# Seven half-size products in place of eight in the last six feed-forward blocks, and a ring of four batches for their input

## The chip, the core and the metric

The kernel runs on one core of a Trainium2 chip. The metric is the device time of one execution in microseconds (us), the median of several runs; the profiled span is about 1.8 us shorter than the time of the same run. A ratio is the mean time of one kernel's runs over the mean of the other's runs of the same rounds, so it isn't quite the ratio of the medians quoted.

PE is TensorE, DVE is VectorE, ACT is ScalarE, POOL is GpSimd and SP is SyncE. SBUF and PSUM are the two on-chip memories; here a PSUM bank holds one result of 128 x 512 fp32. In a line of a profile, `o<-ps_f` means that o is written from ps_f, `L714` is the line of kernel.py, and `[2.70 <-PE ...]` is the idle time before the instruction and what ended it.

## The reference

```python
# attention: batch 8, heads 8, sequence 576, head size 64
scores = scale * np.matmul(q, k.transpose(0, 1, 3, 2))
mask_local = (rel >= 0) & (rel < 32)                        # heads 0 to 3
mask_strided = (rel >= 0) & (pos[None, :] % 32 == pos[:, None] % 32)   # heads 4 to 7
... # softmax over the keys, then
x = np.matmul(attn, v) # as 4608 tokens x 512
# feed-forward: 4608 tokens, model size 512, inner size 2048
h = x @ w_in
r = np.maximum(h, 0.0)
g = s * (r * r) + b
out = g @ w_out           # fp32
```

## The kernel before

The tokens are worked in nine blocks (numbered 0 to 8) of 512. A planner emits the instructions of all engines in one order, and each engine keeps to it: in the traces below a TensorE or VectorE instruction that waits holds up all behind it (5.24 us in one case). The scores and sums of attention are used as filler between feed-forward matmuls. The second product of a block is 64 matmuls of 512 columns. Each 16 of them fill one PSUM bank, VectorE evicts it into one of three output buffers, and SyncE stores that buffer:

```python
op = ctx.enter_context(tc.tile_pool(name="op", bufs=3))      # output buffers, 2 KB a partition each
xT = [const.tile([128, NTOK], FP16, name=f"xT{i}") for i in range(4)]
...
def ff2(T, ts, ft, group, part=0, parts=1):
    ...
        nc.tensor.matmul(
            out=gts[id_], lhsT=gts[T][:, ft, ts * 128:(ts + 1) * 128],
            rhs=w_out_sb[:, ft, cols], start=(ft == 0), stop=(ft == NFT - 1))
    ...
        def ev(eng):
            o = op.tile([128, DM], FP32, tag="o", name="o")
            nc.vector.scalar_tensor_tensor(
                out=o[:, 0:n], in0=gts[id_], scalar=s_sb[:, 0:1], in1=bcs[:, cols],
                op0=ALU.mult, op1=ALU.add)
            r0 = T * PS + ts * 128
            nc.sync.dma_start(out=out[r0:r0 + 128, cols], in_=o[:, 0:n])
```

Attention of a head pair needs q and k transposed, which in the later batches SyncE does by DMA in the same queue as the stores.

The softmax here doesn't subtract the row's maximum and nothing guards it: scores larger than these inputs give would overflow.

## Time and profile before

| | before |
|---|---|
| median of the first 3 runs (a fourth came with the result) | 318.59 us (317.58 to 319.23) |
| profiled span | 315.9 us |
| TensorE busy | 310.1 us, 98% |
| VectorE busy | 194.5 us, 62% |
| granted TensorE clock | 1.00 in every stretch |

A busy share of 98% says that TensorE is nearly always occupied, so the first question for a change is what it does to TensorE's stream of matmuls, and the second is whether any other engine can make TensorE stop. The lines of the page are shown and read in the prediction.

### The profile page before, as it was taken

The page shows a single profiled execution, that of the slowest core. Times are in us where ns is not written, and L with a number is a line of the kernel's source. Part 1 is how long each engine was busy: PE and PEld are TensorE (multiplying, and loading weights), DVE is VectorE, ACT ScalarE, POOL GpSimd, SP SyncE. Part 2 cuts the span into 40 slices and gives each one's busy share as a digit, 9 for nine tenths or more (in the row PEclk, how much of TensorE's full clock was granted, in tenths as well). Part 3 has the DMA queues.
Part 4 walks back from the last instruction along what each step waited for, and adds up shares of the span by engine and source line. Part 5 has one row for each costly group of instructions (what it writes and reads, how often), then busy time and mean ns, then how long its engine had stood idle before and what let it go on. Part 6 is the DMA issues. An engine that isn't in the chain of part 4 may idle for free.

```text
span 315.9 us, 6151 instructions
## 1 busy us (share of the span) xinstructions
PE 310.1 (98%) x2268; PEld 175.2 (55%) x2268; DVE 194.5 (62%) x543; ACT 160.8 (51%) x304; POOL 97.1 (31%) x140
## 2 busy tenths in 40 slices
PE   8999999999999999999999999999999999999995
PEld 3775655666556566556555655565544454544444
DVE  5576868798967797658566877595732254333212
ACT  1776944788838688547037815661531164333100
POOL 8562569902960292059201870000000000000000
PEclk9999999999999999999999999999999999999999
DMA  8999999994999699679997999923050100100021
GB/s 128 206 212 204 212 170 152 233 139 97 78 156 170 84 139 141 129 141 135 159 187 145 122 164 147 165 89 106 19 91 33 66 35 0 66 36 33 33 100 70
DMA packets 99385, 37.83 MB, mean 120 GB/s; under 512 B 82394, under 2 KB 93274, under 8 KB 99354
## 3 DMA queue, kind: packets, MB, share of 16 engines
q0 software_dynamic: 57200, 18.08, 57.8%
q1 hardware_dynamic: 42154, 19.35, 31.5%
q8 instruction: 18, 0.29, 0.4%
q14 instruction: 13, 0.11, 0.1%
HBM read 36.84 MB, written 10.62 MB: 150 GB/s over the span
## 4 chain that ended last, share of the span: by engine, by line
PE 89%; DMA 8%; POOL 1%; issue 0%; SPq 0%; DVE 0%; POOLq 0%
PE ps_f L703 39%; PE ps_f L663 37%; PE ps_s L505 5%; DMA kl<-in_k_dram 4%; PE ps_a L557 4%; DMA w_out_sb<-in_v_dram 2%; DMA ql<-in_q_dram 2%; PE ps_t L387 1%; PE ps_a L726 1%; PE ps_t L605 1%; POOL v_loc L293 1%; PE ps_f L557 0%; SPq L797 0%; POOL ql L251 0%; PE ps_f L387 0%
## 5 line engine op out<-in xcount | busy, mean ns | idle before, releaser
L663 PE MATMUL ps_f<-xT,w_in_sb 128*128 128x512 f16 x568 | 145.7, 379 | 0.0
L703 PE MATMUL ps_f<-w_out_sb,gT 128*128 128x512 f16 (+1 forms) x592 | 144.8, 373 | 0.0
L681 ACT ACTIVATE u<-ps_f 128x512 f16<-128x512 f32 x140 | 82.8, 597 | 98.3 <-PE ps_f L663 85.0
L687 DVE TENSOR_TENSOR gT<-u 128x512 f16<-128x512 f16 x144 | 59.5, 417 | 46.9 <-ACT u L681 46.0
L663 PEld LDWEIGHTS <-w_in_sb 128*128 128x128 f16 x576 | 61.2, 114 | 44.6 <-issue 0.2
L703 PEld LDWEIGHTS <-gT 128*128 128x128 f16 x592 | 55.6, 98 | 52.5 <-DVE gT L687 0.6
L519 ACT ACTIVATE pt<-ps_s 128x384 f16<-128x384 f32 (+2 forms) x92 | 42.0, 490 | 8.1 <-PE ps_s L505 7.3
L714 DVE SCALAR_TENSOR_TENSOR o<-ps_f,s_sb,bcs 128x512 f32<-128x512 f32 (+1 forms) x37 | 27.0, 730 | 25.1 <-PE ps_f L703 24.5
L557 PEld LDWEIGHTS <-pt 72*72 72x72 f16 (+1 forms) x448 | 31.8, 119 | 15.9
L583 DVE TENSOR_TENSOR x_nat<-ps_a,rec 72x256 f16<-72x256 f32 (+1 forms) x76 | 35.0, 460 | 1.3
L572 DVE RECIPROCAL rec<-ps_a 72x4 f32<-72x4 f32 (+1 forms) x76 | 13.8, 181 | 24.3 <-PE ps_a L557 24.1
L271 POOL DMA_DIRECT2D v_loc<-in_v_dram x28 | 20.6, 742 | 3.7 <-DVE qD_loc L293 2.3
L758 POOL COPY gate<-kT 1x1 f16<-1x1 f16 x6 | 1.4, 230 | 47.6 <-DMA kT<-ks 47.6
L527 DVE TENSOR_TENSOR pt<-pt,mask_str 72x432 f16<-72x432 f16 (+1 forms) x42 | 14.6, 356 | 1.8 <-ACT pt L519 1.3
L527 DVE TENSOR_TENSOR pt<-pt,mask_loc 128x384 f16<-128x384 f16 x42 | 14.0, 352 | 2.4 <-ACT pt L519 2.0
L557 PE MATMUL ps_a<-v_str,pt 72*72 72x65 f16 x204 | 15.3, 197 | 0.0
L276 POOL DMA_DIRECT2D v_str<-in_v_dram x16 | 13.0, 816 | 5.6 <-DVE rec L572 2.7
L557 PE MATMUL ps_a<-v_loc,pt 128*96 128x65 f16 x150 | 12.0, 206 | 0.0
L248 POOL DMA_DIRECT2D kl<-in_k_dram x16 | 11.7, 745 | 0.0
L913 PE MATMUL ps_f<-ones 128*128 128x512 f16 (+2 forms) x30 | 9.3, 444 | 1.4 <-DVE ones L226 1.1
L505 PE MATMUL ps_s<-qD_loc,kT_loc 128*128 128x192 f16 x68 | 10.4, 246 | 0.0
L293 ACT COPY xT<-ps_t 128x576 f16<-128x576 f16 x7 | 4.5, 638 | 10.9 <-PE ps_t L605 10.9
(111 smaller groups left out, 242.5 us busy)
## 6 DMA issues: line engine op xcount, KB each, us to landing
out_dram<-o SPq DMA_DIRECT2D x35, 256.0 KB, 4.2
w_out_sb<-in_moe_w_out_dram POOLq DMA_DIRECT2D x4, 512.0 KB, 10.8
v_loc<-in_v_dram POOLq DMA_DIRECT2D x28, 72.0 KB, 7.9
ql<-in_q_dram POOLq DMA_DIRECT2D x6, 288.0 KB, 6.9
qs<-in_q_dram POOLq DMA_DIRECT2D x6, 288.0 KB, 5.1
ks<-in_k_dram POOLq DMA_DIRECT2D x6, 288.0 KB, 6.9
kl<-in_k_dram POOLq DMA_DIRECT2D x4, 288.0 KB, 8.8
kl<-in_k_dram POOLq DMA_DIRECT2D x16, 72.0 KB, 4.0
```

What stands on the lines that cost most here:

```text
L271: nc.gpsimd.dma_start(out=vl[LPAD:128, h, :, 0:D], in_=v_band(b, h))
L505: nc.tensor.matmul(out=st["s", g][0:nk, c:c + 2 * nq], lhsT=(st["k"][:, i * nq:i * nq + nk] if loc else st["k"][:, i, 0:SQ]), rhs=st["q"][ ...
L519: nc.scalar.activation(out=pt[0:nk, 0:2 * n].rearrange("k t c -> k (t c)"), in_=st["s", g][0:nk, 0:2 * n * nq], func=AF.Exp, scale=scale)
L527: nc.vector.tensor_tensor(out=pt[0:nk, 0:2 * n], in0=pt[0:nk, 0:2 * n], in1=mask, op=ALU.mult)
L557: nc.tensor.matmul(out=st["a"][0:nq, j % per, :], lhsT=st["pt", g][0:nk, i, :], rhs=vt[0:nk, 2 * mm + e, j, :])
L572: nc.vector.reciprocal(out=st["rec", e, j][0:nq, 0:per], in_=st["pa", e, j][0:nq, 0:per, D:D + 1])
L583: nc.vector.tensor_tensor(out=st["x"][:, j0:j0 + per, 64 * e:64 * e + 64], in0=st["pa", e, j][0:nq, 0:per, 0:D], in1=st["rec", e, j][0:nq, ...
L663: nc.tensor.matmul(out=gts["h", T, ft], lhsT=w_in_sb[min(ft // 4, 2)][:, ct].rearrange("p (c x l) -> p c l x", x=128, l=4)[:, max(ft // 4 ...
L681: nc.scalar.activation(out=gts["u", T, ft], in_=gts["h", T, ft], func=AF.Relu)
L687: nc.vector.tensor_tensor(out=gts[T][:, ft, :], in0=u, in1=u, op=ALU.mult)
L703: nc.tensor.matmul(out=gts[id_], lhsT=gts[T][:, ft, ts * 128:(ts + 1) * 128], rhs=w_out_sb[:, ft, cols], start=(ft == 0), stop=(ft == NFT ...
L714: nc.vector.scalar_tensor_tensor(out=o[:, 0:n], in0=gts[id_], scalar=s_sb[:, 0:1], in1=bcs[:, cols], op0=ALU.mult, op1=ALU.add)
```

## The change

Strassen's scheme writes a 2 x 2 block product with seven half-size products of sums in place of eight. For each of the last six blocks (3 to 8), the 64 matmuls of 512 columns become 7 x 16 of 256 columns. VectorE pays for it: sums of the activations g (in place, in fp16), four mixings of the weights once, and intermediate values (Va, Ua, Ub, Vb) that are copied out of PSUM between products. To make room in SBUF, the transposed x is kept for four batches in a ring and not for all eight, and some input buffers are shared.

```diff
+    sp = ctx.enter_context(tc.tile_pool(name="sp", bufs=1))
+    cp = ctx.enter_context(tc.tile_pool(name="cp", bufs=1))
+    w_mix = {i: const.tile([128, NFT // 2, DM // 2], FP16, name=f"w_mix{i}") for i in (2, 3, 4)}
-    xT = [const.tile([128, NTOK], FP16, name=f"xT{i}") for i in range(4)]
+    NX = 4
+    xT = [const.tile([128, NX * S], FP16, name=f"xT{i}") for i in range(4)]
...
-                                  bufs=7 if loc else 6, name="pt")
+                                  bufs=6, name="pt")
...
+    SEVEN = 3
+    def sums_post(T):
...
+            plan.post([("S", T, 1, h), ("P1", T)], ns,
+                      make((0, 0), (1, 0), (0, 0), ALU.subtract), [("S", T, 2, h)])
...
+        jobs = ((3, wr[1], wr[0]), (1, wr[0], wl[0]), (2, wr[1], w_mix[1]), (4, wl[1], w_mix[2]))
+        before = [("F2", SEVEN - 1)]
...
+        def store(i, k, of, plus, ts=slice(0, 2)):
+            def g(eng):
+                o = op.tile([128, 2, 256], FP32, tag="o", name="o")
+                nc.vector.scalar_tensor_tensor(
+                    out=o[:, ts], in0=gts[of, T][:, ts], scalar=s_sb[:, 0:1],
+                    in1=plus()[:, ts], op0=ALU.mult, op1=ALU.add)
+                r0 = T * PS + 256 * i
+                nc.sync.dma_start(...)
...
+        seq = [
+            ("P1", X, ..., [([d("P1"), ("bcs",)], EV, ev("Va", "X", lambda: b1), [d("Va")])]),
+            ("P5", W, ..., mix(1), sn(1), wait(1), []),
+            ("P2", X, ..., [d("Va")], [([d("P2")], EV, store(0, 0, "X", lambda: b1), [X])]),
+            ("P6", Y, ..., ev("Ua", ...), add_db -> Ub),
+            ("P7", Z, ..., ev("Vb", ...), store(1, 1, "W", val("Vb"))),
+            ("P4", Z, ..., [d("Vb")] + wait(4), store(1, 0, "Z", val("Ua"))),
+            ("P3", W, ..., [d("C22")], store(0, 1, "W", val("Ub"))),
+        ]
+        if not late:
+            seq = [seq[i] for i in (0, 2, 3, 4, 1, 5, 6)]
```

P1 to P7 are the seven products; C11, C22, C21 and C12 are the four quarters of a block's output, stored in that order. P2 accumulates into the bank that P1 filled, so it can't start before Va has been copied out of it.

## The prediction

> **What bounds the kernel now.** I read the page from the top: busy time of each engine, then the chain that ended last.
>
> ```profile
> PE 310.1 (98%) x2268; PEld 175.2 (55%) x2268; DVE 194.5 (62%) x543; ACT 160.8 (51%) x304; POOL 97.1 (31%) x140
> ...
> PE 89%; DMA 8%; POOL 1%; issue 0%; SPq 0%; DVE 0%; POOLq 0%
> PE ps_f L703 39%; PE ps_f L663 37%; PE ps_s L505 5%; DMA kl<-in_k_dram 4%; PE ps_a L557 4%; DMA w_out_sb<-in_v_dram 2%; DMA ql<-in_q_dram 2%; PE ps_t L387 1%; PE ps_a L726 1%; PE ps_t L605 1%; POOL v_loc L293 1%; PE ps_f L557 0%; SPq L797 0
> ```
>
> 89% of the chain is TensorE; the two feed-forward products are 76% of it, and VectorE has none. A busy PE need not stream, so I looked at the groups of the two products and at the last microseconds in the timeline.
>
> ```profile
> L663 PE MATMUL ps_f<-xT,w_in_sb 128*128 128x512 f16 x568 | 145.7, 379 | 0.0
> ...
> L703 PE MATMUL ps_f<-w_out_sb,gT 128*128 128x512 f16 (+1 forms) x592 | 144.8, 373 | 0.0
> ```
>
> ```profile
> 302.13 0.75 DVE L714 SCALAR_TENSOR_TENSOR o<-ps_f,s_sb,bcs 128x512 f32<-128x512 f32 x1 [2.70 <-PE ps_f L703]
> 305.58 0.75 DVE L714 SCALAR_TENSOR_TENSOR o<-ps_f,s_sb,bcs 128x512 f32<-128x512 f32 x1 [2.70 <-PE ps_f L703]
> 309.04 0.75 DVE L714 SCALAR_TENSOR_TENSOR o<-ps_f,s_sb,bcs 128x512 f32<-128x512 f32 x1 [2.70 <-PE ps_f L703]
> 310.79 0.48 DVE L714 SCALAR_TENSOR_TENSOR o<-ps_f,s_sb,bcs 128x256 f32<-128x256 f32 x1 [1.00 <-PE ps_f L703]
> 312.53 0.48 DVE L714 SCALAR_TENSOR_TENSOR o<-ps_f,s_sb,bcs 128x256 f32<-128x256 f32 x1 [1.26 <-PE ps_f L703]
> ```
>
> The idle column is 0.0: neither product waits. Evictions 3.46 us apart close 16 matmuls of 512 columns each: 216 ns a matmul. The last two are 1.74 us apart and close 16 of 256 columns: 109 ns each, although every one has a new stationary operand. So half-size products cost half. The PE order is therefore a clock: counting matmuls at 216, 109 and the shorter attention sizes gives when each step would run if nothing waited.
>
> Then VectorE by stretch, to see what room it has.
>
> ```profile
> 60.00:80.00 20.00, 20.00 (x181) 12.52 (x180) 17.81 (x49) 16.92 (x34) 6.31 (x10) 1.00 0.97 129
> 120.00:140.00 20.00, 20.00 (x147) 11.21 (x145) 13.61 (x42) 12.18 (x22) 3.25 (x8) 1.00 0.96 130
> 260.00:280.00 20.00, 20.00 (x95) 9.88 (x93) 7.37 (x16) 7.76 (x13) 0.00 (x0) 1.00 0.07 26
> ```
>
> The third figure after the length and the PE is DVE: up to 89% (17.81 of 20) without a PE gap, 68% in the middle, 37% late. The change adds where there is little room (120 to 200 us) as well as where there is much.
>
> Last, the attention cycle, which has one PSUM bank:
>
> ```profile
> 187.11 0.17 DVE L572 RECIPROCAL rec<-ps_a 72x4 f32<-72x4 f32 x1
> 187.32 0.42 DVE L583 TENSOR_TENSOR x_nat<-ps_a,rec 72x256 f16<-72x256 f32 x1
> ```
>
> Attention output takes PE 0.30 us, then 0.17 and 0.42 on DVE with small gaps, before the bank is free: about 1.0 us a group when nothing fills it. Today feed-forward matmuls fill it.
>
> **What the Trainium skill says.** "TensorE: Matmul & The Clock Gate", Back-to-back issue gap: columns/2.4 + 2.5 ns, so 216 at 512 and 109 at 256; the trace agrees exactly. Same page, Part 3, The mechanism: matmuls are strictly in order, so one that waits for a bank holds all behind it; the before trace has no such wait to show it. "VectorE: DVE Perf Modes", The perf-mode tier table: a 16-bit tensor_tensor from SBUF runs two elements a cycle, fp32 or PSUM one. The trace agrees: squares of 512 take 417 ns and masks of 384 take 352, a slope of 0.51 to 0.56 ns an element; the 512-column eviction takes 744.
>
> **The change, part by part.**
>
> PE: six blocks lose 64 x 216 = 13.82 us and get 7 x 16 x 109 = 12.21: 1.62 a block, 9.7 in all. One block's first product straddles the ring of four batches and becomes 128 halves: +0.1. Gain 9.6 us.
>
> DVE: a sum of 1024 fp16 elements is 0.71 us (417 + 512 x 0.56); the trace's adjacent instructions overlap by some 0.07, so it occupies 0.64. Eight a block: 5.1. Seven evictions and one fp32 add (estimate 0.55) in place of four evictions at 0.67 net: 7 x 0.67 + 0.55 - 2.7 = 2.6. Together 7.7 a block, 46 for six. Mixing the weights: four of 2048 elements at 1.22, plus 0.3: 5.2. DVE rises from 194 to about 246 us, some 80%. As a sum it fits. But from the thirteenth square of block 3 to the first of block 5 the changed order holds 155 DVE instructions worth 59 us (35 masks, 25 reciprocals, 25 normalisations, 20 squares, 16 evictions, 14 copies, 13 sums, the mixing) against 58 us of PE stream: no room.
>
> The order of each engine shows where PE then waits. I followed both engines by hand at the durations above, 0.2 us from the end of a matmul's issue to its reader (216 ns of issue show as 379 in the trace, so 0.16, and a semaphore).
>
> - Block 3 begins. The second product accumulates into the bank of the first, whose value must be copied out in between (Va). DVE's order first has one mixing (1.2), the last plain eviction (0.7) and two sums (1.3). P1 issues until t, Va is done at t + 2.8: PE waits 2.5 to 2.9. Two more mixings then stand before the third product: 1.0. Total 3.6.
> - Block 3's rest: filled by the first product of block 4, DVE about 84% loaded: 0.5.
> - Block 4 runs its seven products in one piece, since block 5's input isn't there yet in the order. Va comes after two sums: 0.2 + 1.3 + 0.75 against 0.65 of attention work: 1.6. The bank for the fourth product: 0.3.
> - Then the order has seven attention groups with 2.5 us of PE work and no feed-forward before block 5's first product. At 1.0 us a group plus the masks and copies between them they need 7 to 8: 5.2.
> - Block 5: the second product follows the first with no filler, and two sums and Va stand between: 2.1.
> - Blocks 6 and 7: 2.6 us of filler (twelve matmuls) covers Va, nothing.
> - Block 8, the end: the value of the fifth product in order must leave its bank before the sixth accumulates there: 0.2 + 0.75 = 1.0. The last eviction and store are as before.
>
> Sum of waits 3.6 + 0.5 + 1.9 + 5.2 + 2.1 + 1.0 = 14.3. Net 14.3 - 9.6 = +4.7 us: 323.3. Hand tracing of waits errs upward more often than not (a value may already be out, DVE may start a sum early), so I take 2 us off: 321.5.
>
> **The rivals.**
>
> 1. DVE hides: 80% busy in all, 89% was held in one stretch of before without a gap. Then only the end's 1.0 stays: 318.6 - 9.6 + 1.0 = 310. Against it: the waits above come from banks and order, not from load; they hold even if DVE is idle before them, for a sum and an eviction are longer than the filler.
> 2. Weight loads bound the half-size matmuls. The load takes 98 ns from gT and 114 from w_in. At 114 the 672 would cost 3.4 us more, so 325. Against: the sixteen halves at the end ran at 109, and loads from gT are the common case.
> 3. The sums fall to one element a cycle, through the slices or in-place writing: 48 x 0.5 = 25 us of DVE more, of which maybe 8 are seen: 330. For: no trace instruction has just this shape. Against: masks with a broadcast operand kept the fast rate.
> 4. The ring, the shared buffers (three in place of two and two) and one mask buffer less make loads or transposes late. The new waits on GpSimd and the ring name readers that come several microseconds earlier in the order: nothing, or 1 us.
> 5. PE gaps lower the clock. PEclk is 1.00 in every stretch, also in the first 20 us with PE at 18.05: not expected, or 2 us.
>
> **Range and chances.** The waits could be 9 to 17 us, which gives 318.0 to 326.0; rival 1 in part stretches it down. Range 314 to 327. Faster by 2% (under 312.2) needs waits under 3.2 us: 0.07. Slower by 2% (over 325) needs over 16, or rivals 2, 3: 0.18. Within: 0.75.
>
> **What would show it.** The profile after should have 9.6 us less of matmul stream, and PE idle or a chain with DVE in it, gaps before the second product of blocks 3, 4, 5 for Va, and a stretch of 7 to 8 us before block 5's first product with attention alone. Sums near 0.71 us, L812 matmuls at 109 ns apart, DVE busy near 246. If PE still shows no idle in the middle and the span falls to 307, the hand tracing is wrong and rival 1 right; if sums take 1.1 us, rival 3.

## More of the kernel before

SyncE issues the DMA (transfers) that store the results and, for most batches, transpose q, k and x.

## The result, and the profile after

| | before | after |
|---|---|---|
| median | 318.91 us (317.58 to 319.54) | 331.53 us (330.4 to 332.55) |
| profiled span | 315.9 us | 328.6 us |
| TensorE busy | 310.1 us | 307.4 us |
| VectorE busy | 194.5 us | 241.2 us |
| granted clock, mean | 1.00 | 0.974 |

The ratio is 1.041, with a 95% interval of 1.037 to 1.044: slower by 12.6 us, where an increase of 2.9 was predicted. Executions over 1.5% slower than the fastest of the same kernel are left out of the means. The results are correct.

The page of the changed kernel, busy times, granted clock by slice (in tenths, 40 slices of 8.2 us) and the chain that ended last:

```profile
PE 307.4 (94%) x2604; PEld 211.3 (64%) x2604; DVE 241.2 (73%) x614; ACT 164.0 (50%) x308; POOL 97.5 (30%) x142
PEclk9999999999999999999899998589999999999999
PE 72%; DMA 14%; DVE 6%; POOL 3%; issue 2%; ACT 1%; SPq 0%; DVEq 0%; POOLq 0%
```

TensorE's share of the chain fell from 89% to 72%. DMA and DVE together have 20% where DMA and POOL had 9%. The clock has a dip to 5 tenths at the 26th slice, 205 to 214 us.

The groups of the products and of the new sums (busy us and mean ns of one; then the idle time of the engine before them):

```profile
L841 PE MATMUL ps_f<-xT,w_in_sb 128*128 128x512 f16 (+1 forms) x632 | 146.2, 360 | 0.0
L812 PE MATMUL ps_f<-w_out_sb,gT 128*128 128x256 f16 x384 | 50.7, 276 | 5.1 <-DVE Va L741 4.2
L695 DVE TENSOR_TENSOR gT<-gT 128x1024 f16<-128x1024 f16 x36 | 24.0, 688 | 3.7 <-PE ps_f L812 3.6
```

The sums take 0.688 us (0.71 predicted), so they keep the fast rate. The half products wait 5.1 us in all, nearly all for Va. That was the mechanism predicted, but 5.1 us can't explain 12.6. Next, the windows (length, busy us of PE, weight loads, DVE, ACT, POOL, then granted clock, DMA share and GB/s):

```profile
150.00:160.00 10.00, 8.05 (x67) 6.73 (x65) 10.00 (x17) 0.00 (x0) 3.27 (x5) 0.83 2.02 164
200.00:210.00 10.00, 4.00 (x35) 3.25 (x36) 5.07 (x18) 4.68 (x10) 0.00 (x0) 0.63 0.91 226
210.00:220.00 10.00, 8.51 (x63) 5.36 (x62) 6.52 (x22) 4.35 (x9) 0.00 (x0) 0.69 0.19 47
260.00:280.00 20.00, 20.00 (x130) 13.34 (x128) 12.17 (x24) 8.57 (x15) 0.00 (x0) 1.00 0.08 28
```

In the kernel before, TensorE was full over the same time:

```profile
200.00:220.00 20.00, 20.00 (x139) 11.35 (x138) 13.03 (x36) 9.12 (x20) 0.00 (x0) 1.00 0.49 119
```

The late stretch, 260 to 280, is as full as before. The loss is around 150 to 160 and above all from 200 to 220: TensorE is busy for 4.00 of 10 us, and **VectorE for only 5.07**. If VectorE's load were the limit there, it would be full. Its timeline just before tells why it isn't (start, duration, operation, and in brackets the idle time before it with what ended it):

```profile
195.79 0.75 DVE L752 SCALAR_TENSOR_TENSOR o<-ps_f,s_sb,Vb 128x512 f32<-128x512 f32 x1
...
196.93 0.74 DVE L752 SCALAR_TENSOR_TENSOR o<-ps_f,s_sb,Ua 128x512 f32<-128x512 f32 x1
...
203.95 0.75 DVE L752 SCALAR_TENSOR_TENSOR o<-ps_f,s_sb,Ub 128x512 f32<-128x512 f32 x1 [5.24 <-DMA out_dram<-o]
...
204.82 0.42 DVE L596 TENSOR_TENSOR x_nat<-ps_a,rec 72x256 f16<-72x256 f32 x1
```

VectorE wants to evict C12 of block 4 at about 198.7. All three output buffers are taken, and it stands for 5.24 us until a store has landed. The attention normalisation behind it in VectorE's order (x_nat, at 204.82) stands too, and with it the one attention bank. SyncE's own queue shows the buffer's story; C11 of block 4 had been evicted at 189.32 to 190.06:

```profile
184.51 4.67 SPq L469 DMA_TRANSPOSE qTl<-ql  x2
189.28 0.55 SPq L756 DMA_DIRECT2D out_dram<-o  x1
189.99 4.36 SPq L450 DMA_TRANSPOSE kT_alt<-kl  x2
194.46 3.62 SPq L477 DMA_TRANSPOSE qT<-qs  x2
198.18 0.60 SPq L641 DMA_DIRECT2D x_dram<-x_nat  x1
198.87 0.38 SPq L756 DMA_DIRECT2D out_dram<-o  x1
```

The store at 189.28 is that of the block before. The store of C11 was issued at 198.87, 8.8 us after its data were ready (198.87 - 190.06), behind four transposes and another store. It landed 5.1 us later, at 203.95. In the kernel before, SyncE's queue looks much the same at this time, but evictions come at 182.56, 186.45 and 201.33, so three buffers are plenty.

TensorE in the same time:

```profile
200.98 0.51 PE L518 MATMUL ps_s<-qD_loc,kT_alt 128*128 128x192 f16 x4 [1.92 <-DMA kT_alt<-kl]
...
205.30 0.40 PE L570 MATMUL ps_a<-v_str,pt 72*72 72x65 f16 x4 [3.08 <-DVE x_nat L596]
...
212.46 1.47 PE L841 MATMUL ps_f<-xT,w_in_sb 128*128 128x512 f16 x3
```

The last line is block 5's first matmul of the first product. Block 4's last matmuls had ended at about 198.6, so the attention-only stretch, predicted at 7 to 8 us, took 13.9. Two suspects stand beside the buffer: the transposed k arrives late (1.92), and the clock is lowered. The chain that ended last (`--critical`: start, duration, what) passes through the store and not through the transposed k:

```profile
198.87 4.99 DMA out_dram<-o
...
203.95 0.06 DVE o L752
...
205.30 0.40 PE ps_a L570 x4
```

The 1.92 us lie before the end of the buffer wait and are hidden by it: TensorE stood until 205.30 in any case.

Last, the end of the kernel (VectorE), which answers to the five evictions of before:

```profile
320.82 0.75 DVE L752 SCALAR_TENSOR_TENSOR o<-ps_f,s_sb,Vb 128x512 f32<-128x512 f32 x1
322.78 0.75 DVE L752 SCALAR_TENSOR_TENSOR o<-ps_s,s_sb,Ua 128x512 f32<-128x512 f32 x1 [1.21 <-PE ps_s L812]
323.87 0.48 DVE L752 SCALAR_TENSOR_TENSOR o<-ps_f,s_sb,Ub 128x256 f32<-128x256 f32 x1 [0.34 <-PE ps_f L812]
325.26 0.48 DVE L752 SCALAR_TENSOR_TENSOR o<-ps_f,s_sb,Ub 128x256 f32<-128x256 f32 x1 [0.91 <-PE ps_f L812]
```

In this stretch TensorE waits 0.84 us for Vb (1.0 predicted), and then the last six matmuls of P3 wait 0.58 us for an eviction, which wasn't predicted.

Counting TensorE's order as a clock, as the prediction does, gives where each microsecond was lost (delay that each step adds over the stream of matmuls alone, good to some 0.1 us; it is larger by about 0.16 us than the idle time in the brackets, which starts at the modelled end of the matmul before):

| step | predicted | measured |
|---|---|---|
| block 3 begins | 3.6 | 3.8 (about 0.4 of it lowered clock) |
| block 3's rest | 0.5 | 0 |
| block 4 | 1.9 | 1.8 |
| stretch of attention before block 5 | 5.2 | **11.2** |
| half clock in the first products of block 5 | 0 | 1.9 |
| block 5, wait for Va | 2.1 | 2.04 |
| blocks 6 and 7 | 0 | 0 |
| end | 1.0 | 1.75 |
| sum | 14.3 | 22.5 |

22.5 less the 9.6 of the shorter stream is 12.9, and the spans differ by 12.7. The 0.4 in the first row is a comparison: from block 3's first half product to block 4's first matmul this kernel took 9.07 us, and four_ob below, whose clock stayed at 1.00 there, 8.63. The matmuls themselves were stretched by more, but at full clock they wait for the mixed weights in that time (0.72 us in four_ob).

### The profile page after: what moved, and what is told of

Its sections match the earlier page's. It is cut to its first block, busy times and chain, and to the rows that moved or that the text cites. A ratio compares the mean times of both kernels' runs of the same rounds, so it can differ in the third digit from the quotient of the medians.

```text
span 328.6 us, 6925 instructions
## 1 busy us (share of the span) xinstructions
PE 307.4 (94%) x2604; PEld 211.3 (64%) x2604; DVE 241.2 (73%) x614; ACT 164.0 (50%) x308; POOL 97.5 (30%) x142
## 4 chain that ended last, share of the span: by engine, by line
PE 72%; DMA 14%; DVE 6%; POOL 3%; issue 2%; ACT 1%; SPq 0%; DVEq 0%; POOLq 0%
PE ps_f L841 34%; PE ps_f L812 15%; PE ps_f L887 11%; DMA qs<-in_q_dram 6%; PE ps_a L570 4%; DMA qTl<-ql 3%; PE ps_s L518 3%; DMA w_out_sb<-in_v_dram 2%; DMA ql<-in_q_dram 2%; PE ps_s L812 2%; DMA out_dram<-o 2%; PE ps_t L398 1%; DVE pt L540 1%; PE ps_a L910 1%; DVE x_nat L596 1%
## 5 line engine op out<-in xcount | busy, mean ns | idle before, releaser
L841 PE MATMUL ps_f<-xT,w_in_sb 128*128 128x512 f16 (+1 forms) x632 | 146.2, 360 | 0.0
L841 PEld LDWEIGHTS <-w_in_sb 128*128 128x128 f16 x640 | 68.5, 114 | 35.1 <-issue 0.7
L812 PEld LDWEIGHTS <-gT 128*128 128x128 f16 x576 | 56.4, 99 | 19.2 <-issue 7.0
L812 PE MATMUL ps_f<-w_out_sb,gT 128*128 128x256 f16 x384 | 50.7, 276 | 5.1 <-DVE Va L741 4.2
L887 PE MATMUL ps_f<-w_out_sb,gT 128*128 128x512 f16 x192 | 51.0, 379 | 0.0
L695 DVE TENSOR_TENSOR gT<-gT 128x1024 f16<-128x1024 f16 x36 | 24.0, 688 | 3.7 <-PE ps_f L812 3.6
L887 PEld LDWEIGHTS <-gT 128*128 128x128 f16 x192 | 17.3, 98 | 14.2 <-DVE gT L869 0.6
L570 PE MATMUL ps_a<-v_str,pt 72*72 72x65 f16 x204 | 16.1, 204 | 5.8 <-DVE x_nat L596 5.8
L812 PE MATMUL ps_f<-w_mix,gT 128*128 128x256 f16 x160 | 21.1, 277 | 0.0
L812 PE MATMUL ps_f<-w_mix,S 128*128 128x256 f16 x80 | 12.1, 272 | 0.0
```

Source lines behind the costliest of these rows:

```text
L570: nc.tensor.matmul(out=st["a"][0:nq, j % per, :], lhsT=st["pt", g][0:nk, i, :], rhs=vt[0:nk, 2 * mm + e, j, :])
L695: nc.vector.tensor_tensor(out=at(out), in0=at(x), in1=at(y), op=op)
L812: nc.tensor.matmul(out=gts[name, T][:, t], lhsT=lhs(k, t), rhs=rhs(k), start=fresh and t == k == 0, stop=t == 1 and k == H - 1, skip_group ...
L841: nc.tensor.matmul(out=gts["h", T, ft][:, lo:hi], lhsT=w_in_sb[min(ft // 4, 2)][:, ct].rearrange("p (c x l) -> p c l x", x=128, l=4)[:, ma ...
L887: nc.tensor.matmul(out=gts[id_], lhsT=gts[T][:, ft, ts * 128:(ts + 1) * 128], rhs=w_out_sb[:, ft, cols], start=(ft == 0), stop=(ft == NFT ...
```

## The experiments

The theory after reading the trace: the wait for an output buffer is what made the stretch before block 5 some 6 us too long. The rivals: VectorE's load and order (Va), the late transposes, the ring, and the lowered clock. The before kernel ran beside each (medians of 318.4 to 319.1). Diffs are against the changed kernel.

### ring_only: the ring and the shared buffers without the seven products

```diff
-    SEVEN = 3
+    SEVEN = 99
...
-            mix_post()
+            if SEVEN < NBLK:
+                mix_post()
```

> All nine blocks by plain products, with the ring of four batches, the shared buffers and the smaller mask pool of the changed kernel. My theory (the loss is made of waits around the seven products): same as before, 318.9 us plus 0.1 for the block that straddles the ring, ratio 0.997 to 1.005. Rival (the ring and the shared buffers delay loads and transposes): ratio over 1.01, 322 us or more, with PE gaps near 200 us.

Measured: 318.98 us, ratio 1.001 (0.998 to 1.004). The ring, the shared buffers and the missing mask buffer cost nothing; all that was lost comes from the products and their evictions. The prediction's fourth rival is out.

### va_first: copy Va before the two sums

```diff
-            plan.post([("S", T, 1, h), ("P1", T)], ns,
+            plan.post([("S", T, 1, h), ("P1", T), ("Va", T)], ns,
```

> The changed kernel with the two sums after the first product placed behind the copy Va that frees the bank for the second product. Theory (the gap before the second product is the order on DVE): gaps of 1.95, 0.38 and 1.89 us shrink by up to 1.3 each, with less lowered clock after the first: 328, 327 to 329.5. Rival (DVE load is what counts, the sums have to be done before the next product anyhow): the wait moves to the third product, 330.5 or more.

Measured: two of the four runs fell in the slow state. The two fast ones took 324.11 and 326.28 us, ratio 1.021 (1.016 to 1.026). The profiled run is a slow one, so I use only its order of waits, not its time. In it P2 of block 3 waits 0.84 us for Va (1.95 in the changed kernel), and the product after it, P6, waits 1.92 us for the mixed weights; block 5 waits 0.36 (1.89). The wait for Va is real and partly curable by order, but in block 3 the mixing takes its place. The fast runs are below the 327 expected and gain some 6 us over the changed kernel, as much as free_out below, which is more than the shorter waits for Va explain. The slow trace still has waits of 3.49 and 0.34 us for an output buffer; what the fast runs did isn't shown, and with two runs I draw nothing more from them.

### stores_pool: the block stores from GpSimd's queue

```diff
-                nc.sync.dma_start(
+                nc.gpsimd.dma_start(
```

> The changed kernel with the stores of the seven-product blocks issued from GpSimd's queue instead of SyncE's; the order of PE, DVE and ACT is identical. Theory (the 5.2 us in which DVE waits for an output buffer at 198.8 us come from its store standing in SyncE's queue behind the transposes, and what follows is attention alone at a lowered clock): that wait goes, 331.5 becomes 325, 323 to 327. Rival (attention waits there for the transposes of q and k themselves, or for DVE's load): 330 or more.

Measured: 338.56 us, ratio 1.062: worse. The stores left the transposes' queue for GpSimd's, which also loads q, k and v: there they stand behind those loads, and the loads behind stores that wait for their evictions. VectorE's timeline of this kernel:

```profile
192.51 0.75 DVE L752 SCALAR_TENSOR_TENSOR o<-ps_f,s_sb,bcs 128x512 f32<-128x512 f32 x1 [3.58 <-DMA out_dram<-o]
209.02 0.75 DVE L752 SCALAR_TENSOR_TENSOR o<-ps_f,s_sb,Ub 128x512 f32<-128x512 f32 x1 [6.31 <-DMA out_dram<-o]
```

One wait of 5.24 became two, 9.9 us in all. That fits the theory (longer buffer waits, longer time), but the edit didn't remove what it meant to remove, so it doesn't prove it.

### in_place: two of the four results are evicted into Ua and Ub

```diff
-                o = op.tile([128, 2, 256], FP32, tag="o", name="o")
+                o = gts[into, T] if into else op.tile([128, 2, 256], FP32, tag="o", name="o")
# C21 with into="Ua", C12 with into="Ub"
```

> The changed kernel, but two of the four results of a seven-product block are written over the values Ua and Ub that they are made of and stored from there, so only two a block go through the three output buffers. Order of PE, DVE and ACT unchanged. Theory (the 5.2 us wait of DVE at 198.8 us is for an output buffer, and GpSimd's queue was only a worse place for the stores): that wait goes with part of the lowered clock after it: 331.5 becomes 325, 323 to 327. Rival (attention there waits for the transposes in SyncE's queue; the buffer wait is beside it): 329.5 or more.

Measured: 333.33 us, ratio 1.043 (1.035 to 1.051), not better, which is what the rival had said, but for another reason. The wait moved to the tiles that now are the buffers:

```profile
192.88 0.75 DVE L741 SCALAR_TENSOR_TENSOR Ua<-ps_f,s_sb,Va 128x512 f32<-128x512 f32 x1 [2.44 <-DMA out_dram<-Ua]
199.51 0.69 DVE L763 TENSOR_TENSOR Ub<-Ua,bcs 128x512 f32<-128x512 f32 x1 [5.41 <-DMA out_dram<-Ub]
```

Ub and Ua exist once each, so the next block's Ub must wait for this block's store, and TensorE waits 1.84 and 5.15 us behind it.

### from_six: only the last three blocks in seven products

```diff
-    SEVEN = 3
+    SEVEN = 6
```

> Seven products in the last three blocks only (6, 7, 8), where attention is over. Theory: 3 x 1.62 less matmul time, against some 2.5 to 3.5 us of gaps when block 6 begins with the mixing and 1.7 at the end: 319, 317 to 321. Rival (each seven-product block costs more than it saves, 12.6/6 = 2.1 us net): 325.

Measured: 317.83 us, ratio 0.997 (0.993 to 1.000). With attention out of the way by block 6, the loss is gone. One wait for Va of 2.09 us remains in block 6, and the end's 0.84 and 0.58. Three blocks save 3 x 1.62 = 4.9 us of stream; about 1 us of it arrives.

### warm, warm_only: dummy matmuls in TensorE's planned gaps

```diff
-        elif i1 >= 16 or not keep_running(plan.next_time()):
+        elif 16 <= i1 < 256 or not keep_running(plan.next_time()):
# warm: on in_place; warm_only: on the changed kernel
```

> in_place with dummy matmuls in PE's planned gaps from block 4 on (the kernel's own filler of the start, now used later too). Theory (after gaps the granted clock falls, 0.63 to 0.83 in three stretches of the changed kernel, and matmuls then take longer): clock 0.99 to 1.00 and 2 to 4 us less than in_place, about 322. Rival (the waits alone count, the lowered clock falls in time that is idle anyway): within 1 us of in_place, or slower by the fillers.

> The changed kernel with dummy matmuls in the planned PE gaps from block 4 on, the stores as they were. Theory (the lowered clock alone costs 3 us): 328 to 329, granted clock above 0.99. Rival (warm gained over in_place through its other timing of stores): 330 or more.

Measured: warm 327.80 us, ratio 1.028 (1.024 to 1.032); warm_only 327.36 us, ratio 1.028 (1.023 to 1.033). Both are 4 to 5.5 us better than their base, with a mean clock of 0.992 or more. This looked as if the lowered clock were a 4 us cause of its own. The trace of warm_only (its slowest run, only 1.1 us shorter than the changed kernel's) shows two things. The wait for an output buffer is 1.87 us and not 5.24, but the buffer came free at nearly the same time, 203.66 against 203.95: VectorE only came to it later, at about 201.8 and not 198.7, since block 3 began 2.4 us later and dummy matmuls took time besides. Block 5 began no earlier (212.70, against 212.46). What this trace gained came after that: from there to the same half product of block 5's second product (223.54 and 224.96) TensorE took 10.84 us at full clock, and 12.50 in the changed kernel at half clock. So some 1.7 us of the clock's cost is real; how the rest of the 4 us arose, the trace doesn't show.

### stores_act, act_warm: the block stores from ScalarE's queue

```diff
-                nc.sync.dma_start(
+                nc.scalar.dma_start(
# act_warm: with the dummy matmuls too
```

> The changed kernel with the seven-product stores issued from ScalarE's queue; PE, DVE, GpSimd order unchanged. Theory (the output buffers come free late because their stores stand in SyncE's queue behind the transposes of q and k; in_place only moved the same wait to Ua and Ub): DVE's wait on an output store falls from 5.2 us to under 1, and the time from 331.5 to 326 or 327 (the transposes for block 5's attention and the lowered clock stay). Rival (the transfers themselves are slow whichever queue issues them): a wait of 4 us or more stays, time 330 or more.

> Both: stores from ScalarE's queue and dummy matmuls. Theory: the two gains add, 323 to 324.5, which is what the prediction's waits give without its 2 us of discount (323.3). Rival (they overlap): 326 or more.

Measured: 336.77 us (one of its four runs slow; the fast ones 333.99 to 337.10), ratio 1.060 (1.055 to 1.066), and 338.05 us, ratio 1.061 (1.056 to 1.066). VectorE no longer waits for a store in stores_act, and a store now lands 3.0 us (median) after its issue, not 5.3. But now ScalarE holds at a store until the eviction is there:

```profile
186.62 5.83 ACTq L756 DMA_DIRECT2D out_dram<-o  x3
192.50 1.31 ACT L532 ACTIVATE pt<-ps_s 72x432 f16<-72x432 f32 x3 [7.40 <-DVE rec L585]
```

The exponentials of attention stand 7.40 us behind three stores. The list of this kernel's waits has "ACT u <- DMA out_dram<-o" with 9.0 us. In act_warm VectorE waits 4.9 us for a buffer as well. Once more the wait was moved and not removed.

### best5, best6: what the readings suggest

```diff
-    SEVEN = 3
+    SEVEN = 6                                  # best5: 5
# in_place, and Va before the sums in blocks below 6
-        before = [("F2", SEVEN - 1)]           # mixing of the weights
+        before = [("h", SEVEN, 3)]             # 3, 2 and 4 earlier; 1 last, after Va
-        late = T >= NBLK - 1                   # four PSUM banks for the products
+        late = T >= 6
+        else:                                  # order P1 P7 P6 P2 P5 P4 P3
+            seq = [seq[i] for i in (0, 4, 3, 2, 1, 5, 6)]
```

> A version meant to beat both: seven products from block 5 on; in_place; three of four mixings moved ahead of the block's own products and the fourth behind Va; Va ahead of the sums in block 5; from block 6 on four banks (the score banks, free by then) and the order P1 P7 P6 P2 P5 P4 P3, which puts other products between each product and the next in its bank. Theory: 4 x 1.62 less matmul time, about 1 to 2 us of waits left in block 5: 314, 312.5 to 316. Rival (DVE load in block 5, where attention of batch 7 still runs, gives it back): 317 or more.

> The same from block 6 on, all three blocks with four banks. Theory: 3 x 1.62 less, 0.5 us of waits at the end and at the start of block 6: 314.7, 313.5 to 316; from_six without these gave 317.8. Rival (the gaps are DVE load, not banks and order): 317 or more.

Measured: best5 318.43 us, ratio 0.997 (0.992 to 1.002), outside the 312.5 to 316 expected and in the rival's range, with waits left in block 5 (0.84 for Va, 1.24 for x_nat). best6 314.54 us, **ratio 0.985 (0.981 to 0.989)**, correct: it beats both kernels, if by less than 2%. One gap of TensorE is left after 145 us, at the end:

```profile
308.70 0.81 PE L816 MATMUL ps_f<-w_out_sb,gT 128*128 128x256 f16 x6 [0.58 <-DVE Ub L754]
```

There is no wait of VectorE for a store. The 4.8 us gained (1.5% of 319; the interval is 3.6 to 6.0) agree with the 4.9 us of stream that three blocks save. Where next to nothing waits, the arithmetic of the matmuls comes out. best6 changes four things at once (in_place, the mixing, the banks, the order), and no run tells which of them removed the waits of from_six.

### free_out, free_out_warm: stores that hold no buffer

```diff
                nc.sync.dma_start(
                    out=...,
-                   in_=o[:, ts])
+                   in_=bcs.rearrange("p (t m) -> p t m", t=2)[:, ts] if T in (3, 4)
+                   else o[:, ts])
# free_out_warm: with the dummy matmuls too
```

The stores of blocks 3 and 4 send the bias tile: as many bytes on the same queue, but wrong data in those rows.

> The four stores of blocks 3 and 4 send the finished bias tile to the output instead of the evicted one (wrong in those rows on purpose): same bytes, same queue, same place in the queue, but the output buffers come free without a transfer, so VectorE can't wait 5.24 us for one. Theory (the wait for an output buffer is what makes the attention-only stretch before block 5 6 us longer than predicted): that wait is gone and no other engine takes it over, 325 to 327 us, ratio 1.02 to 1.026. Rival A (the q/k transposes, which come late in SyncE's queue, set the pace of that stretch; the buffer wait is beside it): the wait is gone from the list, the scores of block 5's heads still wait for kT_alt or qT, 329 us or more, ratio over 1.032. Rival B (the lowered clock costs most of it): clock stays at 0.63 to 0.7 between 200 and 220 us, ratio over 1.032, and only the kernel with dummy matmuls gains.

> The same with dummy matmuls in TensorE's planned gaps. Theory, with the lowered clock as a second and separate part of 4 us: 322 to 324 us, ratio 1.01 to 1.018, about what was predicted for the change (321.5). Rival A: 326 to 328 us, no better than dummy matmuls alone (327.36). Rival B: as much better than free_out as dummy matmuls alone were than the changed kernel or more (4 us), free_out itself little better than the changed kernel.

Measured: free_out 325.45 us, ratio 1.021 (1.018 to 1.024): 6.1 us less than the changed kernel, inside the 325 to 327 that the theory gave. VectorE evicts C12 at 198.24 without a wait. Block 5's first matmul starts at 206.51 (212.46 in the changed kernel):

```profile
206.51 1.47 PE L843 MATMUL ps_f<-xT,w_in_sb 128*128 128x512 f16 x3
```

free_out_warm took 327.03 us, ratio 1.024 (1.021 to 1.028). The fillers bring nothing once the buffer wait is gone. So of the theory's two claims the first held and the second, 4 us more from the clock, fell. That doesn't make the lowered clock free: block 5's first products run at half clock in free_out too, and in free_out_warm they are faster but begin 4.2 us later (210.73), so what the fillers give they also take.

One flaw remained. These stores don't wait for an eviction, so SyncE's queue ran ahead and issued kT_alt's transposes at 182.59 us, not 189.99. The gain could have come from earlier transposes.

### four_ob: a fourth output buffer, queue unchanged

```diff
-    op = ctx.enter_context(tc.tile_pool(name="op", bufs=3))
+    op = ctx.enter_context(tc.tile_pool(name="op", bufs=4))
...
-            gts["Ub", T] = cp.tile([128, 2, 256], FP32, tag="Ub", name="Ub")
+            gts["Ub", T] = gts["Ua", T]
```

Ub is written over Ua, which makes one quarter of each block wrong and frees the 2 KB for a fourth buffer. (With Ub kept in a tile of its own, a fourth buffer doesn't fit in SBUF and the kernel doesn't build.)

> The sum Ub is written over Ua instead of into a tile of its own (on purpose one quarter of each block's outputs then has a bias difference too much), and the 2 KB a partition that this frees make a fourth output buffer. Every store still reads its evicted tile, so SyncE's queue keeps its order and its waits, and the q/k transposes stay as late as in the changed kernel; only the wait for a free output buffer is relaxed. Theory (the buffer wait is the 6 us): VectorE's wait on a store is gone or under 1 us, 325 to 327 us, ratio 1.019 to 1.027, as with free_out (325.45). Rival A (free_out gained because its stores no longer held up the queue, so that the transposes came up to 7 us earlier): the buffer wait is gone but PE waits for kT_alt or qT instead, 329 us or more, ratio over 1.032.

Measured: 326.78 us, ratio 1.027 (1.025 to 1.030), within the theory's range in time and at its upper edge in ratio. SyncE and VectorE in four_ob:

```profile
189.10 4.10 SPq L450 DMA_TRANSPOSE kT_alt<-kl  x2
...
197.38 0.38 SPq L756 DMA_DIRECT2D out_dram<-o  x1
```

```profile
198.03 0.75 DVE L752 SCALAR_TENSOR_TENSOR o<-ps_f,s_sb,Ua 128x512 f32<-128x512 f32 x1 [0.21 <-PE ps_f L812]
```

The transposes are as late as in the changed kernel (189.10), the store of C11 is issued as late (197.38), and yet VectorE evicts C12 at once, having waited only for its matmuls. The stretch from block 4's last matmul to block 5's first took 10.6 us (8.6 in free_out, 13.9 in the changed kernel). The whole kernel gained 331.53 - 326.78 = 4.8 us (4.3 between the means). Not all of that is the buffer: of the 4.5 us between the two profiled spans, 3.3 lie in the stretch, 0.8 came before block 4's end and 0.4 after block 5's first matmul. And the first scores of the stretch, which waited 1.92 us for kT_alt in the changed kernel, started at once here (198.01), so kT_alt landed sooner after its issue; that wait was hidden behind the buffer's, but it would have shown once the buffer wait was gone. The other 1.3 us of free_out's 6.1 appear only when the transposes come early too. The waits that are left in four_ob are 0.57 us for kT_alt, 1.15 for qT and 2.51 of TensorE for x_nat, and its chain in this stretch passes through the transposes of q:

```profile
193.30 9.32 DMA qT<-qs
```

So with the buffer wait gone, the late transposes (rival A) are the next limit.

## Why the prediction was right or wrong

**Right: the stream.** best6 got 4.8 us (3.6 to 6.0) from three blocks where 4.9 were computed, so 1.62 a block holds within the noise and with it the 9.6. Rival 2 (weight loads) is out: sixteen halves in the changed kernel take 1.75 us (188.60 to 190.35), 109 ns each.

**Right: VectorE's costs.** Sums at 0.688 us against 0.71, busy 241.2 us against 246 (which is 77% of 321.5, not the "some 80%" of the text). Rival 3 is out.

**Right: the waits for banks and their order.** Block 3 lost 3.8 against 3.6 (3.3 in four_ob at full clock), block 5 2.04 against 2.1, blocks 6 and 7 nothing, the end's Vb 1.0 on the same count as predicted. Rival 1, that VectorE hides, was false, as argued. Block 3's rest, put at 0.5, cost nothing. In block 4 only the sum agrees, 1.8 against 1.9, and that is luck: about 1.1 was lost before P2, where 1.6 was predicted for Va, the fourth product had its bank at once, and 0.5 was lost before P3, because VectorE waited 0.50 us for a transpose of q before it evicted C22.

**Wrong: "At 1.0 us a group plus the masks and copies between them they need 7 to 8: 5.2."** This is the step that failed. The stretch took 13.9 us and added 11.2. The hand tracing followed TensorE and VectorE with PSUM banks only; it left out the output buffers and the queue of their stores. "As a sum it fits", and 16 evictions were counted, but not where each one's buffer came from. The new scheme makes three quarters of block 4 due within 3 us (195.79, 196.93 and about 198.7), while SyncE's queue is full of transposes. The mechanism missed is a wait for a free output buffer, 5.24 us in the trace; with a fourth buffer the stretch is 10.6 us, and with stores that hold none and a queue that runs ahead it is 8.6, nearly what was predicted.

**Wrong: "PE gaps lower the clock ... not expected, or 2 us."** The clock did fall, to 0.63 and 0.69 in the stretches from 200 to 220 and to 0.83 at 150 to 160. It cost some 0.4 us at the start of block 3 and 1.9 at the start of block 5, besides what it cost inside the stretch. That is the 2 us that the rival allowed and a little more, and it should have been in the sum, for a predicted stretch of 7 us with 2.5 us of work is just such a gap. PEclk had been 1.00 in a kernel without such gaps, which says nothing of one with them. The lowered clock follows the waits; dummy matmuls in the gaps didn't recover it in free_out_warm, where they cost as much as they gave.

**Wrong: "so I take 2 us off".** The sum without it was 323.3 (less 2 it is 321.3; the text has 321.5). The first products of block 5 at half clock (1.9) and the missed 0.75 us at the end (1.75 against 1.0) bring it to 326.0; free_out measured 325.45. So for the kernel without the buffer wait the working was within some 2 us even before the clock, in part because errors cancel: it had 1.3 us too much in blocks 3 and 4 (0.3, 0.5 and 0.5) and some 1 us too little in the stretch. The discount went the wrong way: on balance hand tracing had missed waits, not invented them.

**Open.** Why the dummy matmuls gained 4.2 us in the changed kernel and nothing in free_out isn't settled, nor why Va first gained some 6 us in its two fast runs. How the 4.3 to 4.8 us of four_ob divide between the free buffer and the sooner landing of kT_alt isn't either. The changed kernel with nothing but a fourth buffer added doesn't fit in SBUF, and no correct kernel with six blocks and four buffers was run.

## What to carry to other kernels

When a change makes results come due in bursts, follow the output buffers as you follow the banks: for each eviction, ask which store must have landed, and what stands before that store in its queue. A wait that is moved to another queue or tile was still a wait on some engine here; only a further buffer, stores that hold none, or no such block while the queue is full, took it away. In this kernel the scheme paid only in the blocks where attention was over: three blocks, with their order arranged anew, gave 4.8 us, six cost 12.6.

## What the Trainium skill lacked or had wrong

- "DMA: Bandwidth & Descriptors", Issuing engines are not separate DMA queues, says that issuing from several engines saves only the issuing time, "which is usually small relative to the DMA itself". Here the queue ahead of one store was larger than its transfer: 8.8 us behind four transposes and a store, then 5.1 us to land. Nor does the page warn that a store on ScalarE's queue holds its activations until the data are ready: 7.40 us here, though stores then landed in 3.0 us.
- "TensorE: Matmul & The Clock Gate", Why this matters for your kernels, advises no TensorE gap above some 3 us. Around a gap of 1.95 us the granted clock was 0.83 between 150 and 160 us in the changed kernel; gaps of 1.91 (free_out) and 2.09 us (four_ob) at the same place left it at 1.00. In from_six a gap of 2.09 us was followed by 0.50 between 249 and 251 us. So a gap below the limit can cost or not. That would fit the page's own remark on a free-running window (What's actually happening), which the advice leaves out; no run here tests it.
- The same page, Back-to-back issue gap, calls its formula the isolated case and gives 131 ns a matmul at 512 columns as the sustained figure. Here 16 in a row took 3.46 us, 216 ns each, sustained over the span, which is the formula.
- No page that I read has a rule for how many output buffers a burst of evictions needs. Here a fourth buffer gained 4.3 to 4.8 us, of which 3.3 lay in the stretch where the third ran out.
